# Batch 2 loaded six tokens to a partition and turned on TensorE, batch 4's output turned by the crossbar, an own buffer for one pair's exponentials

## The chip, the cores and the metric

The kernel runs on one core of one Trainium2 chip. Its metric is device time in microseconds (us), the median of several executions. A core has five engines that run their own instruction streams and wait for each other through semaphores: PE (TensorE, matrix products), ACT (ScalarE, activation functions), DVE (VectorE, elementwise work), POOL (GpSimd, here casts and some transfers) and SP (SyncE, here transfers only). Data lies in on-chip memory of 128 partitions; matrix products write to PSUM, 8 banks of 512 fp32 numbers in each partition. Sixteen DMA engines carry out the transfers that SP, ACT and POOL issue.

## The reference

Attention that is causal by blocks of 64 tokens, followed by a feed-forward part with a Swish that has a factor for each of its 2048 channels. There are 8 batches, 8 heads, 576 tokens and a head size of 64:

```python
scores = scale * np.matmul(q, k.transpose(0, 1, 3, 2))
mask = block_i >= block_j                      # blocks of 64 positions
scores = np.where(mask, scores, -1e9); scores -= np.max(scores, axis=-1, keepdims=True)
attn = np.exp(scores); attn /= np.sum(attn, axis=-1, keepdims=True) + 1e-09
x = np.matmul(attn, v).transpose(0, 2, 1, 3).reshape(4608, 512)
h = x @ w_in                                   # 4608 x 2048
out = (h / (1 + np.exp(-beta * h))) @ w_out    # 4608 x 512, fp32
```

Inputs and output are fp32; the kernel computes its products in bf16. Swish is computed as 0.5 h (1 + tanh(beta h / 2)).

## The kernel before

**Two parts, woven together.** Attention works in units of one pair of heads of one batch: 32 units, pair `u = 4 b + c`. The feed-forward part works in nine blocks of 512 tokens (`r` = 0 to 8): for each of 16 groups of 128 channels four products with w_in (line 752), a tanh on ACT (line 762) and one DVE operation that makes `gT` (line 766); then four rows of 128 tokens of 16 products with w_out each (line 785), a scaled copy on ACT (line 797) and a store issued by ACT. A block needs the attention of all its tokens: block 0 that of batch 0, block 4 (tokens 2048 to 2559) that of batches 3 and 4.

**One unit of attention.** The scores are computed transposed, keys in partitions, in four groups (line 620): the two heads use the two halves of PE at the same time. ACT takes the exponentials of each group into a buffer `E` (lines 628 and 640), DVE zeroes the masked corners (634 and 636). Thirty products (664) multiply by V, which has a column of ones that gives the sum. DVE takes the reciprocal (676) and normalizes into `xq` (683). The result, tokens in partitions, must be turned into `xT`, channels in partitions: for batches below `XB` by five PE transposes (708) and copies from PSUM on DVE, for two units of batch 0 on ACT (716 and 718); for batches from `XB` on by DMA transposes through the crossbar, issued on SP (696).

**How Q and K come in.** Both must be turned too, and there are two ways, chosen by `QB`. Batches below `QB` (0 and 1) are loaded with six consecutive tokens to a partition, 96 partitions, one transfer for Q and one for K of each pair (line 545). POOL casts them to bf16 (552), PE turns them in six transposes of 96 columns each (561), and a DVE copy puts the columns in token order (569). Later batches are loaded two pairs at a time, 128 tokens to a step in pieces of 256 bytes (lines 580 and 583, five transfers each for Q and K), cast by POOL (591), and turned by one DMA transpose on SP for the two pairs together (598). V is loaded for a whole batch in six transfers (490 and 493) and cast by POOL (505).

**Weights.** w_in and w_out come in four pieces each, by transfers that POOL issues and that cast to bf16 on the way (lines 451 and 456). These stand in POOL's stream between its casts.

**The order.** Nothing is scheduled on the chip. `Plan.schedule` takes all operations with a duration, dependences, a priority and the buffers they need, runs a list scheduler over them in Python, and writes one fixed stream for each engine with the semaphore waits that the dependences need. Priority is lowest number first; `pr(u)` for attention and `1000 + 100 r` for the feed-forward part make PE fall back on w_in and w_out products when no attention is ready. Buffers are given in the order of that schedule: `E` has three (`NE`), so unit 3 takes the one that unit 0 has finished with; `xq` has two, `QKT` three, `ST` (loaded Q or K) six. Of the PSUM banks, 0 to 3 serve pairs of scores and products with V, 4 to 7 all single-bank work. Products on an identity matrix (469 and 471) fill PE where the plan sees it idle in the first 50 us. SP's stream is a queue too: a transfer that waits for an engine holds all transfers behind it.

Of the kernel before, what the change touches and what calls it, by code (L numbers as in the profile page):

```python
# [338 lines left out]
def bass_blockwise_causal_attn__then__act_swish_beta_kernel(  # L339
# [10 lines left out]
    with es:  # L350
        def sb(name, shape, dt):
            return es.enter_context(nc.sbuf_tensor(name, shape, dt))

        NQ = 2
        QB, XB, CAST = 2, 5, "POOL"
# [10 lines left out]
        Ef = [sb(f"E{i}", [128, 3200], bf16) for i in range(NE)]  # L366
        E3 = [e[:, 0:3072].rearrange("p (c h n) -> p c h n", c=3, h=2) for e in Ef]
# [11 lines left out]
        gT = [sb(f"gT{i}", [128, NJ, RC], bf16) for i in range(2)]  # L379
# [8 lines left out]
        for c, n in (("ST", NS), ("QKn", NQ), ("V", NQ), ("Vs", NQ), ("QKT", 3), ("E", NE), ("inv", 3), ("xq", 2),  # L388
                     ("th", 3), ("gT", 2), ("ost", 3)):
            P.slots(c, n)  # L390
# [7 lines left out]
        def dve_t(n):  # L398
            return (n + 125) / 0.96

# [31 lines left out]
        for i in range(NQ, NE):  # L432
            ones.append(P.op("POOL", 100, mk(lambda g, i=i: g.memset(Ef[i][:, 3136:3200], 0.0)), prio=-4))
# [14 lines left out]
        for a in range(4):  # L448
            def fwi(g, e, a=a):
                n = slice(512 * a, 512 * a + 512)  # L450
                return [g.dma_start(w_in[:, :, n], moe_w_in[:, n].rearrange("(c p) n -> p c n", p=128))]

            win.append(P.op("POOL", 1000, fwi, xfer=3150, dma=(f"d_win{a}", 1), prio=-38.5 if a < 1 else -33.2 if a < 2 else -32))
# [75 lines left out]
        for u in range(NU):  # L529
# [73 lines left out]
            te = P.tile("E")  # L603
            ex = []
            zs = []
            for g0 in range(4):
# [19 lines left out]
                if g0 < 3:  # L626
                    def fe(g, e, ps=ps, g0=g0, te=te):
                        return g.activation(E3[te.slot][:, g0, :, :], PS[:, ps.slot:ps.slot + 2, :], ACT.Exp,  # L628
                                            scale=0.125)
                    x = P.op("ACT", act_t(1024), fe, deps=[o], tiles=[ps, te], lat=act_t(1024) + 93, prio=0)  # L630

                    def fz(g, e, g0=g0, te=te):
                        if g0 < 2:
                            return g.memset(E3[te.slot][64:128, g0, :, 0:64], 0.0)  # L634
                        a = E3[te.slot][64:128, 2, :, 0:64]
                        return g.memset(bass.AP(a.tensor, a.offset, [a.ap[0], [512, 2], [320, 2], [1, 64]]), 0.0)  # L636
                    zs.append(P.op("DVE", 160 if g0 < 2 else 220, fz, deps=[x], tiles=[te], prio=-20))
                else:
                    def fe(g, e, ps=ps, te=te):
                        return g.activation(E4[te.slot][:], PS[:, ps.slot, 0:64], ACT.Exp, scale=0.125)  # L640
                    x = P.op("ACT", act_t(64), fe, deps=[o], tiles=[ps, te], lat=act_t(64) + 93, prio=0)
# [3 lines left out]
            def eblk(te, t, i, h):  # L645
                if t == 4:
                    a = 3072
                elif t == 0 and i == 4:
                    a = 1024 + 512 * h + 448
                else:  # L650
                    g0, off = {0: (0, 0), 1: (1, 0), 2: (2, 0), 3: (2, 320)}[t]
                    a = 1024 * g0 + 512 * h + off + 128 * i - 128 * t
                return Ef[te.slot][:, a:a + 128]
# [13 lines left out]

            av = P.op("PE", 30 * 34, fav, deps=ex + zs + [load[u]], tiles=[te, Tv, pv, ti, tx],
# [72 lines left out]
        for r in range(NRC):  # L741
# [5 lines left out]
            for j in range(NJ):  # L747
# [20 lines left out]
                gs.append(P.op("DVE", dve_t(512), fg, deps=[a], tiles=[ph, tt, tg], prio=0))  # L768
# [107 lines left out]
```

## Time and profile before

| what | us |
|---|---|
| median of 5 executions | 354.76 |
| lowest and highest | 353.71 and 356.17 |
| the profiled execution | 353.5 |
| its span, first to last instruction | 351.7 |
| PE busy | 338.6 (96%) |
| ACT busy | 212.0 (60%) |
| DVE busy | 163.2 (46%) |
| POOL busy | 76.5 (22%) |

The profiled execution is one run among others, 1.3 us under the median. "Busy" of PE contains the fillers on the identity matrix and the overlap of products that follow each other, so that it is not a measure of useful work. Rows in order of time give the start, the duration, the engine, the line of the code and, in brackets, the idle time before and what ended it; "xN" merges N equal instructions. A row with a product fewer than the code has is one whose record is missing.

### The profile page before, as it was taken

How to read it: one execution, taken by the hardware profiler on the slowest of the kernel's cores; microseconds unless marked ns; L12 is line 12 of the kernel's file. 1: busy time of each engine (PE TensorE's matmuls, PEld its weight loads, DVE VectorE, ACT ScalarE, POOL GpSimd, SP SyncE). 2: the span in 40 equal slices, each digit the busy share in tenths (PEclk: the TensorE clock that was granted, in tenths of full speed). 3: DMA queues.
4: the chain of work that ended last, by engine and by line, in shares of the span. 5: the costliest groups of instructions: out<-in, count | busy, mean ns of one | idle time of the engine just before them, and what ended most of it. 6: DMA issues, size and time to landing. Idle time of an engine off the chain costs nothing.

```text
span 351.7 us, 6855 instructions
## 1 busy us (share of the span) xinstructions
PE 338.6 (96%) x2767; PEld 170.6 (49%) x2811; DVE 163.2 (46%) x367; ACT 212.0 (60%) x315; POOL 76.5 (22%) x107
## 2 busy tenths in 40 slices
PE   7898999999999999999999999999999999999997
PEld 5474455435455454445444445444444444444444
DVE  3658694038234565137721474137704803812720
ACT  2937962387476897198872977299616715724721
POOL 7386161053242053151023111400000000000000
PEclk9999999999999999999999999999999999999999
DMA  8999999999999999996679996761111011012003
GB/s 213 215 214 250 208 192 211 242 217 210 201 233 210 219 188 211 230 257 121 136 168 170 193 198 138 184 137 36 32 63 60 0 62 60 0 44 77 1 7 115
DMA packets 146672, 52.05 MB, mean 148 GB/s; under 512 B 134720, under 2 KB 142160, under 8 KB 146640
## 3 DMA queue, kind: packets, MB, share of 16 engines
q1 hardware_dynamic: 137088, 37.97, 53.2%
q10 hardware_dynamic: 5328, 9.44, 7.5%
q0 software_dynamic: 4224, 4.19, 7.3%
q8 instruction: 22, 0.36, 0.4%
q14 instruction: 10, 0.08, 0.1%
HBM read 36.71 MB, written 9.44 MB: 131 GB/s over the span
## 4 chain that ended last, share of the span: by engine, by line
PE 90%; DVE 4%; ACT 2%; issue 2%; POOL 0%; POOLq 0%
PE PS L785 36%; PE PS L752 34%; PE PS L620 8%; PE PS L664 7%; PE PS L708 2%; DVE xq L683 2%; PE PS L469 2%; DVE gT L766 1%; PE PS L471 1%; ACT th L762 1%; ACT E L628 1%; PE PS L561 1%; DVE QKT L569 1%; DVE inv L676 0%; ACT xT L716 0%
## 5 line engine op out<-in xcount | busy, mean ns | idle before, releaser
L752 PE MATMUL PS<-xT,w_in 128*128 128x512 bf16 x550 | 129.4, 379 | 3.7 <-issue 1.0
L766 DVE SCALAR_TENSOR_TENSOR gT<-th,PS 128x512 bf16<-128x512 f32 x144 | 97.0, 684 | 75.4 <-ACT th L762 74.5
L785 PE MATMUL PS<-w_out,gT 128*128 128x512 bf16 (+1 forms) x574 | 129.2, 374 | 1.6 <-issue 1.1
L762 ACT ACTIVATE th<-PS,beta 128x512 f32<-128x512 f32 x144 | 98.0, 706 | 25.4 <-PE PS L752 23.5
L628 ACT ACTIVATE E<-PS 128x1024 bf16<-128x1024 f32 x96 | 96.4, 1038 | 24.1 <-PE PS L620 24.0
L785 PEld LDWEIGHTS PS<-w_out,gT 128*128 128x128 bf16 x592 | 55.1, 98 | 63.5 <-issue 4.5
L752 PEld LDWEIGHTS PS<-xT,w_in 128*128 128x128 bf16 x576 | 52.5, 98 | 64.4 <-DVE gT L766 2.6
L797 ACT ACTIVATE ost<-PS 128x512 f32<-128x512 f32 (+1 forms) x37 | 21.7, 588 | 78.9 <-PE PS L785 78.8
L591 POOL CAST QKn<-ST 128x640 bf16<-128x640 f32 x48 | 34.6, 721 | 49.4 <-DMA ST<-in_k_dram 27.7
L620 PE MATMUL PS<-QKT 64*128 64x320 bf16 (+5 forms) x384 | 39.1, 281 | 1.1 <-DVE xq L683 0.5
L505 POOL CAST Vn<-Vs 128x2560 bf16<-128x2560 f32 (+1 forms) x11 | 19.1, 1740 | 85.4 <-DMA Vs<-in_v_dram 85.3
L664 PEld LDWEIGHTS PS<-Vn,E 128*128 128x128 bf16 x960 | 32.5, 97 | 6.8 <-ACT E L640 0.4
L664 PE MATMUL PS<-Vn,E 128*128 128x65 bf16 x960 | 34.1, 193 | 0.5 <-ACT E L640 0.3
L634 DVE MEMSET E<- 64x64 uint32 x64 | 7.1, 112 | 52.4 <-ACT E L628 50.8
L620 PEld LDWEIGHTS PS<-QKT 64*128 64x128 bf16 (+1 forms) x384 | 13.3, 95 | 29.5 <-issue 13.5
L683 DVE TENSOR_TENSOR xq<-PS,inv 128x640 bf16<-128x640 f32 x32 | 26.3, 823 | 0.9
L569 DVE COPY QKT<-PS 128x576 bf16<-128x576 bf16 x16 | 12.0, 755 | 6.1 <-PE PS L561 6.0
L676 DVE RECIPROCAL inv<-PS 128x10 f32<-128x10 f32 x32 | 7.0, 218 | 15.3 <-PE PS L664 15.0
L552 POOL CAST QKn<-ST 96x768 bf16<-96x768 f32 x14 | 11.8, 846 | 5.0 <-DMA ST<-in_k_dram 3.3
L718 DVE COPY xT<-PS 128x64 bf16<-128x64 bf16 (+2 forms) x40 | 9.6, 286 | 6.3 <-PE PS L708 6.1
L636 DVE MEMSET E<- 64x128 uint32 x32 | 5.3, 165 | 14.3 <-ACT E L628 13.3
L708 PE MATMUL PS<-identB,xq 128*128 128x128 bf16 (+1 forms) x100 | 10.5, 216 | 0.4 <-DVE xq L683 0.2
(33 smaller groups left out, 60.2 us busy)
## 6 DMA issues: line engine op xcount, KB each, us to landing
out_dram<-ost ACTq DMA_DIRECT2D x35, 256.0 KB, 2.4
Vs<-in_v_dram SPq DMA_DIRECT2D x28, 256.0 KB, 4.0
ST<-in_q_dram SPq DMA_DIRECT2D x48, 128.0 KB, 3.1
ST<-in_k_dram SPq DMA_DIRECT2D x48, 128.0 KB, 3.3
ST<-in_q_dram SPq DMA_DIRECT2D x8, 288.0 KB, 5.4
ST<-in_k_dram SPq DMA_DIRECT2D x8, 288.0 KB, 6.3
w_in<-in_moe_w_in_dram POOLq DMA_DIRECT2D x4, 512.0 KB, 11.6
w_out<-in_moe_w_out_dram POOLq DMA_DIRECT2D x4, 512.0 KB, 10.3
```

Source lines behind the costliest of these rows:

```text
L505: return g.tensor_copy(Vn[t.slot][:, :, g0:g1, 0:64], Vs[ts.slot][:, :, g0:g1, :])
L591: return g.tensor_copy(QKn[tn.slot][:].rearrange("p a w n -> p (a w n)")[:, 640 * (2 * a + w):][:, 0:640] .rearrange("p (t h d) -> p t h d ...
L620: z = g.matmul(o, QKT[tqk.slot][r, p, 1, 128 * t:128 * t + m], QKT[tqk.slot][r, p, 0, q0:q1])
L628: return g.activation(E3[te.slot][:, g0, :, :], PS[:, ps.slot:ps.slot + 2, :], ACT.Exp, scale=0.125)
L664: z = g.matmul(o, eblk(te, t, i, h), Vn[Tv.slot][:, t, 2 * c + h, 0:65], start=(t == 0), stop=(t == i))
L683: return g.tensor_tensor(xq[tx.slot][:].rearrange("p i (h d) -> p h i d", h=2), both(pv, 0, 64), x, ALU.mult)
L708: z = g.transpose(PSb[:, px.slot, 128 * i:128 * i + r], xq[tx.slot][0:r, i, :], identB[0:r, 0:r])
L752: z = g.matmul(PS[:, ph.slot, :], w_in[:, c, 128 * j:128 * j + 128], xT[:, c, row % RX:row % RX + RC], start=(c == 0), stop=(c == 3))
L762: return g.activation(th[tt.slot][:], PS[:, ph.slot, :], ACT.Tanh, scale=beta[:, j:j + 1])
L766: return g.scalar_tensor_tensor(out=gT[tg.slot][:, j, :], in0=th[tt.slot][:], scalar=1.0, in1=PS[:, ph.slot, :], op0=ALU.add, op1=ALU.mult)
L785: z = g.matmul(PS[:, po.slot, 0:d1 - d0], gT[tg.slot][:, j, 128 * w:128 * w + 128], w_out[:, j, d0:d1], start=(j == 0), stop=(j == NJ - 1))
L797: return g.activation(ost[to.slot][:, 0:n], PS[:, po.slot, 0:n], ACT.Copy, scale=0.5)
```

## The change

`QB` goes from 2 to 3: batch 2 is loaded and turned like batches 0 and 1. `XB` goes from 5 to 4: the output of batch 4 is turned by DMA transposes. Batch 4's tokens wrap around the ring `xT`, so that each of its units is turned in three pieces. Unit 3 gets its exponentials into a buffer of a new class `EX`, which is the storage of the second `gT`, not used before block 1; the DVE operations of block 1 that write `gT` depend on unit 3's users. The second piece of w_in loses its own priority and is issued with the third and fourth.

```diff
-        QB, XB, CAST = 2, 5, "POOL"
+        QB, XB, CAST = 3, 4, "POOL"
...
+        gT = [sb(f"gT{i}", [128, NJ, RC], bf16) for i in range(2)]
+        Ef.append(gT[1][:].rearrange("p j n -> p (j n)")[:, 0:3200])
...
+        def es_(te):
+            return NE if te.cls == "EX" else te.slot
...
-            win.append(P.op("POOL", 1000, fwi, ..., prio=-38.5 if a < 1 else -33.2 if a < 2 else -32))
+            win.append(P.op("POOL", 1000, fwi, ..., prio=-38.5 if a < 1 else -32))
...
-            te = P.tile("E")
+            te = P.tile("EX" if u == 3 else "E")
...
-                return Ef[te.slot][:, a:a + 128]
+                return Ef[es_(te)][:, a:a + 128]
...
+            if u == 3:
+                spare = te
...
-                gs.append(P.op("DVE", dve_t(512), fg, deps=[a], tiles=[ph, tt, tg], prio=0))
+                gs.append(P.op("DVE", dve_t(512), fg, deps=[a] + (spare.users if r == 1 else []),
+                               tiles=[ph, tt, tg], prio=0))
```

The other lines of the diff index the buffer through `es_`, and POOL zeroes the tail of one buffer more. The plan then makes a new order on every engine. On PE 48 transposes of Q and K are added and 20 of outputs leave; on DVE 8 copies of `QKT` are added and 12 copies of `xT` leave; on SP 12 output transposes are added and two of Q and K leave.

## The prediction

> **What bounds the kernel now.** I read the page's busy times first, then busy time by stretch, then TensorE in order of time, then the waits.
>
> From the page and the busy times by stretch (columns: busy us and instructions of each engine, granted clock, DMA share, GB/s):
>
> ```profile
> PE 338.6 (96%) x2767; PEld 170.6 (49%) x2811; DVE 163.2 (46%) x367; ACT 212.0 (60%) x315; POOL 76.5 (22%) x107
> ...
> 48.73:67.25 18.52, 17.64 (x204) 10.34 (x205) 7.71 (x21) 5.80 (x9) 2.29 (x4) 1.00 1.17 217
> ...
> 119.33:131.00 11.67, 10.82 (x107) 5.55 (x109) 7.32 (x19) 11.33 (x19) 5.20 (x5) 1.00 1.13 214
> ```
>
> TensorE is the bound: 96% busy over the span and 17.64 of 18.52 us even where batch 1 ends, at granted clock 1.00, so I weigh an edit by the TensorE time it adds or takes. Only two things lie outside: the front, before the first product with w_in, and single holes. The DMA engines are full (a share over 1.0), though, so what arrives late there can become a hole. In 119 to 131 ScalarE is busy 11.33 of 11.67 us: there it is nearly the bound.
>
> The front, TensorE and the others in order of time (start, duration, engine, line, count, idle before and what ended it):
>
> ```profile
> 18.00 1.50 POOL L505 CAST Vn<-Vs 128x640 bf16<-128x640 f32 x2 [4.62 <-DMA Vs<-in_v_dram]
> 18.61 1.72 PE L471 MATMUL PS<-identF,identB 64*64 64x256 bf16 x28
> 20.26 1.08 PE L664 MATMUL PS<-Vn,E 128*128 128x65 bf16 x30
> 20.46 0.74 POOL L451 DMA_DIRECT2D w_in<-in_moe_w_in_dram  x1 [0.96 <-DMA Vs<-in_v_dram]
> 21.20 1.52 POOL L505 CAST Vn<-Vs 128x640 bf16<-128x640 f32 x2
> 21.37 0.22 ACT L640 ACTIVATE E<-PS 128x64 bf16<-128x64 f32 x1 [3.74 <-PE PS L664]
> 21.49 2.85 ACT L628 ACTIVATE E<-PS 128x1024 bf16<-128x1024 f32 x3
> 29.25 0.81 PE L752 MATMUL PS<-xT,w_in 128*128 128x512 bf16 x3 [0.41 <-ACT xT L716]
> ```
>
> ScalarE idles 3.74 us until the first product with V (20.26) has freed pair 0's buffer of exponentials, and only then does pair 3's. The first w_in product starts at 29.25.
>
> **The change part by part.** The profiled execution took 353.5 us around a span of 351.7; the median of the five is 354.76, 1.3 above. I work in differences and put them on the median.
>
> *Prices of TensorE blocks*, by the distance of starts in the same order of time:
>
> ```profile
> 33.42 0.43 PE L561 MATMUL PS<-identB,QKn 96*128 96x96 bf16 x6
> 33.69 1.03 PE L752 MATMUL PS<-xT,w_in 128*128 128x512 bf16 x3
> ...
> 70.70 1.03 PE L752 MATMUL PS<-xT,w_in 128*128 128x512 bf16 x4
> 71.56 1.03 PE L785 MATMUL PS<-w_out,gT 128*128 128x512 bf16 x4
> 72.52 0.79 PE L620 MATMUL PS<-QKT 64*128 64x512 bf16 x10
> ...
> 77.66 0.39 PE L620 MATMUL PS<-QKT 64*128 64x448 bf16 x4
> 77.98 1.90 PE L752 MATMUL PS<-xT,w_in 128*128 128x512 bf16 x8
> ...
> 88.57 0.52 PE L708 MATMUL PS<-identB,xq 128*128 128x128 bf16 x5
> 89.02 1.25 PE L785 MATMUL PS<-w_out,gT 128*128 128x512 bf16 x5
> ```
>
> Four products of 512 columns cost 0.86 us (70.70 to 71.56), 0.96 where scores follow (71.56 to 72.52): 0.10 for the turn. Four score products in two halves, 512 columns of stream or 0.215 us, take 0.32 (77.66 to 77.98): 0.11 more. So each visit to the scores costs 0.21 us over its stream. Six transposes of 96 columns cost 0.27, five of an output 0.45.
>
> *Batch 2 turned on TensorE.* Eight groups of six: 8 x 0.27 = +2.2 us, all on the bound, with no cover. *Batch 4's output off it:* 4 x 0.45 = -1.8. *The order:* the plan writes 64 visits to scores after the first w_in product instead of 70: 6 x 0.21 = -1.3. The last counts only if the new visits price like the old; where a visit follows an output's transposes the turn is mostly hidden already (seven such before, four after), so the bound towards nothing is +0.7 and the sum of the three lies between -0.9 and -0.2. I take -0.9, since most visits have the full price.
>
> [...]
>
> *Pair 3's own buffer.* Its exponentials no longer wait for the product at 20.26; they follow pair 2's, which end at 17.63, and are done about 21.1. The second w_in piece moves behind the V casts on POOL, so those end at 20.46 + 1.52 = 22.0 instead of 22.72. Written out by the new order with durations from the rows: products with V of pairs 0 and 1 20.4 to 22.3 (24 fillers instead of 28, one score group more), transposes of pair 0 after its normalization (0.22 + 0.82) to 23.1, pair 2 to 24.0, transposes to 24.5, pair 3 to 25.4, transposes to 25.9, eleven fillers of 0.11 to 27.1, last transposes to 27.5, ScalarE's copy (0.71) to 28.4. First w_in product 28.4 instead of 29.25: -0.85. Bounds: -1.3 if the fillers weren't in the way, 0 if something else holds that product. What is late next: w_in's second piece. Issued at 20.46, at the median landing of w_in (11.6 us) it was there at 32.1 and moves by 1.5; its first user stands near 36.5, so nothing.
>
> *VectorE.* 8 copies of 0.757 more, some 2.7 us of output copies fewer. Four copies (3.0 us) fall at 51 to 56 us between normalizations and output copies, whose users are TensorE's transposes. VectorE is busy only 7.71 of 18.52 us there, but in a chain: last g at 49.7, normalizations (1.04 each) to 51.9, two copies to 53.4, output copies to 54.6. TensorE reaches pair 4's output transposes at 50.4 and waits to 50.9, about 0.5 us. Before, one hole of 0.7 stood at the same place (50.64 to 51.71 for one score group). I count both alike: 0, between -0.7 and +1.
>
> *POOL.* Eight casts of 0.82 for eight of 0.72: +0.8 in 76 us of work. But four of them now stand ahead of three w_out pieces, which so start at 49.3 instead of 45.91 (V of batch 1 cast until 46.0, then 4 x 0.82). The time from issue to landing of w_out's pieces (smallest, median, largest) is in the view of line 456:
>
> ```profile
> DMA to landing us min/median/max: 6.5/10.3/14.3
> ```
>
> The last, issued at 47.4, so landed about 61.7 and would land at 65.1. Its first user stands at 69.5 by my block sums: over 4 us of cover, cost 0; a rival below is what happens without it.
>
> *SP's queue.* 16 loads of 0.51, 4 of 0.60 and 2 turns of 3.93 go (18.5 us of issue), 8 loads of 0.44 and 12 output turns of 1.23 come (18.3). The output turns wait for VectorE, and loads of batches 5 and 6 stand behind them; but those are issued some 20 us ahead of need. The reader of batch 4's rows, the fifth block of 512 tokens, starts near 191, turned at 125 to 149. Cost 0, at most a hole of a few tenths.
>
> *ScalarE.* Same instructions, but products with w_in and scores are packed closer in blocks 1, 3 and 4, while the w_out stretches get longer. 119 to 131 is the row for a dense stretch: the one hole in it was 0.69 us. I take as many holes after as before: 0, between -1.5 and +1.5.
>
> Sum: -0.9 - 0.85 = -1.75, to which a tenth for the lost hole at 30.9 (QKT waits) brings it to -1.85: a profiled time of 351.65, and 354.76 - 1.85 = **352.9 us**. A change under 0.5% (1.8 us) can hardly be told from none in this kernel.
>
> **The rivals.**
>
> *Gain eaten by new holes (same).* The order is planned with given durations; ScalarE's 1038 ns for 1024 columns must then fit by chance. For it: the new order packs blocks 3 and 4 as 119 to 131 is packed now. Against: the stretch with block 5, already so packed (230 to 252), loses only half a microsecond. One hole of 0.7 in each of blocks 1, 3 and 4, less the one that goes at 127: -1.85 + 1.4 = 354.3.
>
> *The edit is empty in front (same).* If the first w_in product waits for something common to both, -0.85 goes: 353.8. For it: TensorE has fillers there, so the place isn't bound by itself. Against: both ScalarE's 3.74 us and the cast order are seen as waits.
>
> *w_out comes late (slower).* The six-token loads of pairs 10 and 11 may share the engines with the three w_out pieces. TensorE's order is fixed, so a late piece stops everything behind it. The last is issued at 50.8, and it decides once it lands after 69.5, that is 18.7 us after issue; every microsecond beyond counts whole. For it: w_in's last piece, beside the six-token loads of batch 1, took 15.3 us instead of 14.3, and the engines were full at 48 to 67 us. At 15.3 there is no hole; at 22 the hole is 3.3 us and the kernel takes 356.2; at twice 14.3 it is 10 us and 362.8. Against: in SP's order V of batch 2 stands before those loads, so most of them come after w_out.
>
> **How the numbers follow.** The sum as worked out, faster: 0.46, own range 350.4 to 353.0. Same, by holes or an empty front: 0.34, 353.0 to 356.2. Late w_out or a like hole: 0.20, 356.2 to 362.8, more likely near the lower end. The low end is every term at its good bound: -0.9 - 1.3 - 0.7 - 1.5 = -4.4, 350.4. The high end, 357.0, takes in the two middle cases and a late piece of up to 2 us.
>
> **What would show it.** The first w_in product at 28.4; ScalarE without a wait of 3.7 us before L640's line; eight more groups of transposes at 0.27; waits of TensorE for the w_out pieces absent (they would disprove the cover); holes after scores in blocks 1, 3 and 4 under 0.7 each. A clock below 1.00, or TensorE waiting for DMA at 60 to 75 us, would make the prediction wrong.

## The result, and the profile after

The changed kernel takes 357.69 us (median of 20 executions, 355.69 to 360.81) where the kernel before takes 354.38 us in the runs beside it: a ratio of 1.0095, with a 95% interval of 1.0076 to 1.0115. It is slower by 0.9%, the sign and the range of the forecast were both missed, and the loss is about twice the half per cent that can just be told from none.

What an execution takes goes with its mean granted clock (the share of full clock that the profile says TensorE was given), which in the profiled one fell by a stretch at half clock (0.50 over 209.85 to 213.20 us, mean 0.995): of the 20, the nine at 0.999 or more have a median of 356.4 us, the other eleven of 358.8; of 88 executions of the kernel before beside the experiments below, 64 and 24, with medians of 354.1 and 356.0. So the change costs 2.3 us where the mean clock is 0.999 or more, and a lower one came more often with it (11 of 20 against 24 of 88).

The profiled execution took 359.43 us around a span of 357.6, that is 5.9 us more than the profiled one of before (353.5); it is 1.7 us above its kernel's median, that one 0.9 below. The page's busy times, granted clock by slice and DMA share by slice:

```profile
PE 341.7 (96%) x2801; PEld 174.1 (49%) x2844; DVE 165.0 (46%) x363; ACT 211.6 (59%) x315; POOL 77.1 (22%) x108
...
PEclk9999999999999999999999989999999999999999
DMA  8979899999898973948899796860121011002003
```

TensorE is still 96% busy and still the bound, but one slice (the 24th, 206 to 215 us) has a clock below full, and the DMA engines, busy from the start, show two dips between 134 and 161 us (a 3 and a 4); before, no slice ahead of 158 us is under 8. (The changed kernel's line numbers are five to seven higher: its lines 625, 669, 759 and 792 are 620, 664, 752 and 785 before, its 603 and 703 are 598 and 696.)

**Where the time went.** I priced every TensorE block after the first w_in product by the prediction's prices (0.216 us a product of 512 columns, 0.265 six transposes of Q and K, 0.09 an output transpose, 0.905 the thirty products with V of a pair, a visit to the scores 0.11 plus a change-over of 0.10, which the prediction calls the turn) and compared the sum with the time from the first w_in product to the last block of w_out. Where scores follow an output's five transposes, the two together cost 0.22 us less: 0.32 or 0.33 from the start of the transposes to that of the scores, where the prices would give 0.45 and 0.10. Two rows of the kernel before:

```profile
128.08 0.52 PE L708 MATMUL PS<-identB,xq 128*128 128x128 bf16 x5
128.40 0.63 PE L620 MATMUL PS<-QKT 64*128 64x320 bf16 x6
```

What the sum leaves over I call holes. The sum is thus counted from the order and priced; only its difference from the measured time is read off the trace.

| profiled execution | first w_in product | sum of blocks | holes | start of the last block |
|---|---|---|---|---|
| before | 29.04 | 300.76 | 5.25 | 335.05 |
| after | 30.72 | 300.48 | 9.81 | 341.01 |

(The first w_in product stands 0.216 us ahead of its first row, since that product's record is missing in both profiles.) So +1.68 us in front, -0.28 in the blocks and +4.56 in holes. The new holes lie in one place. TensorE in order of time there:

```profile
203.16 2.54 PE L759 MATMUL PS<-xT,w_in 128*128 128x512 bf16 x11 [0.16 <-DVE inv L683]
205.54 1.07 PE L669 MATMUL PS<-Vn,E 128*128 128x65 bf16 x30
209.25 0.54 PE L625 MATMUL PS<-QKT 64*128 64x512 bf16 x4 [2.65 <-DMA QKT<-QKn]
209.72 1.84 PE L759 MATMUL PS<-xT,w_in 128*128 128x512 bf16 x4
211.78 1.49 PE L759 MATMUL PS<-xT,w_in 128*128 128x512 bf16 x3 [0.22 <-issue]
```

The scores of pair 26 wait 2.65 us for the Q/K turn, as I call the DMA transpose of Q and K for two pairs (`QKT<-QKn`; an output turn is `xT<-xq`). Then four products of w_in take 1.84 us, nearly twice their usual time (1.03 us for four in the prediction's rows). The two stretches of that place, with the clock ahead of the DMA share:

```profile
200.00:210.00 10.00, 7.19 (x89) 4.19 (x88) 6.58 (x14) 6.57 (x10) 2.88 (x4) 0.99 0.95 197
210.00:220.00 10.00, 9.78 (x51) 3.77 (x51) 3.74 (x10) 8.21 (x14) 0.00 (x0) 0.84 0.95 152
```

The granted clock is 0.84 over 210 to 220 and 0.99 over the 10 us ahead of it; over 209.85 to 213.20 it is 0.50. That makes about 3.4 us of half clock (0.16 and 0.01 of 10 us, at one half). It costs another 1.87 us of holes. Without it, and without the later start that is explained below (1.35), the two profiles are 2.7 us apart, near the 2.3 between the executions at full clock. The gap of 2.65 us was followed by half clock here, and a gap of 2.71 us in another execution of the same kernel (below) was not (granted clock 1.00 from 205 to 220 us); in the run of batch 2 alone (below) one of 2.25 us was (0.50 from 219.30 to 222.60).

Why the turn was late stands on SyncE's queue (issue time, its length, line, count; the second column is how long the issue held the queue):

```profile
130.15 9.62 SPq L703 DMA_TRANSPOSE xT<-xq  x6
139.81 3.09 SPq L603 DMA_TRANSPOSE QKT<-QKn  x1
...
150.86 7.68 SPq L703 DMA_TRANSPOSE xT<-xq  x6
158.59 2.57 SPq L585 DMA_DIRECT2D ST<-in_k_dram  x4
...
197.12 3.30 SPq L585 DMA_DIRECT2D ST<-in_q_dram  x4
200.46 0.62 SPq L588 DMA_DIRECT2D ST<-in_q_dram  x1
201.12 2.25 SPq L585 DMA_DIRECT2D ST<-in_k_dram  x4
203.42 0.60 SPq L588 DMA_DIRECT2D ST<-in_k_dram  x1
204.06 3.46 SPq L603 DMA_TRANSPOSE QKT<-QKn  x1
```

Batch 4's twelve output turns hold SyncE for 17 us in two stretches. In them the DMA engines have less to do: their share is 0.16 over 130 to 140 and 0.41 over 150.86 to 158.54. The turn that pair 26 needs is issued at 204.06 and lands at 209.21; in the kernel before it went out at 198.37 and landed at 204.29, ahead of its first user at 208.22. It is the queue that holds it: POOL's last cast for it ends at 197.61, when SyncE has just begun on the ten loads of the next two pairs (197.12 to 204.02); it issues them one after the other and only then comes to this turn.

The Q/K turns of both kernels, by pairs, show how SyncE's lead came and went (issue time, us):

| pairs | 12, 13 | 14, 15 | 16, 17 | 18, 19 | 20, 21 | 22, 23 | 24, 25 | 26, 27 |
|---|---|---|---|---|---|---|---|---|
| before | 87.64 | 106.77 | 111.73 | 133.67 | 138.38 | 158.12 | 171.64 | 198.37 |
| after | 78.49 | 98.40 | 104.05 | 124.68 | 139.81 | 168.90 | 176.11 | 204.06 |

Up to 125 us the changed kernel is 8 to 9 us ahead, by the issues of batch 2 that it saves SyncE. The output turns use that up and more. Busy times by stretch, of the kernel before:

```profile
100.00:160.00 60.00, 58.15 (x558) 29.57 (x568) 29.10 (x84) 42.77 (x63) 19.04 (x22) 1.00 1.04 220
160.00:260.00 100.00, 98.32 (x855) 48.12 (x869) 47.59 (x110) 67.76 (x100) 14.72 (x16) 1.00 0.63 130
```

And of the changed kernel, the same two stretches:

```profile
100.00:160.00 60.00, 58.89 (x508) 29.21 (x517) 25.58 (x64) 37.20 (x54) 12.37 (x13) 1.00 0.81 168
160.00:260.00 100.00, 95.23 (x816) 47.17 (x826) 45.59 (x106) 68.32 (x104) 17.60 (x20) 0.98 0.72 151
```

The last two columns are the DMA share and GB/s. Before, loads fill the DMA engines until 160 us (1.04, 220 GB/s) and so run ahead of TensorE. After, the share is 0.81 and 168 GB/s there, and loads that were not issued there fall behind 160 us (0.72 and 151 GB/s against 0.63 and 130).

**The front.** The wait of 3.74 us on ScalarE is gone, as forecast (its rows of after):

```profile
18.88 0.22 ACT L645 ACTIVATE gT<-PS 128x64 bf16<-128x64 f32 x1
18.98 2.11 ACT L633 ACTIVATE gT<-PS 128x1024 bf16<-128x1024 f32 x2
```

Yet the first w_in product comes at 30.94 instead of 29.25. TensorE's rows of after:

```profile
5.98 0.69 PE L566 MATMUL PS<-identB,QKn 96*128 96x96 bf16 x6
...
21.83 1.98 PE L669 MATMUL PS<-Vn,E 128*128 128x65 bf16 x60
...
25.07 1.08 PE L669 MATMUL PS<-Vn,E 128*128 128x65 bf16 x30 [0.46 <-DVE xq L690]
...
30.34 0.28 PE L474 MATMUL PS<-identF,identB 128*128 128x256 bf16 x1 [0.33 <-ACT xT L723]
30.94 0.81 PE L759 MATMUL PS<-xT,w_in 128*128 128x512 bf16 x3
```

The first six transposes take 0.69 us at 5.98; in the kernel before they took 0.42 at 5.71. TensorE began this execution more slowly (why is not seen: the granted clock reads 1.00 in both from 5 to 12 us), so that the first scores start at 9.35 instead of 8.00. That is 1.35 of the 1.68 us, and no matter of the change: the profiled executions of all kernels here have their first scores anywhere between 7.96 and 9.35, with the change and without. From the first product with V to the first w_in product it is 9.11 us, before 8.99. The own buffer has given nothing there.

### The profile page after: what moved, and what is told of

Same layout as the page of the kernel before. It is cut to its first block, busy times and chain, and to the rows that moved or that the text cites. A ratio compares the mean times of both kernels' runs of the same rounds, so it can differ in the third digit from the quotient of the medians.

```text
span 357.6 us, 6931 instructions
## 1 busy us (share of the span) xinstructions
PE 341.7 (96%) x2801; PEld 174.1 (49%) x2844; DVE 165.0 (46%) x363; ACT 211.6 (59%) x315; POOL 77.1 (22%) x108
## 4 chain that ended last, share of the span: by engine, by line
PE 79%; DVE 7%; SPq 6%; ACT 4%; issue 2%; DMA 2%; POOL 0%; ACTq 0%; POOLq 0%
PE PS L792 31%; PE PS L759 30%; PE PS L625 6%; PE PS L669 6%; SPq L585 3%; DVE gT L773 2%; SPq L703 2%; PE PS L474 2%; DVE QKT L574 2%; ACT E L633 2%; DVE xq L690 2%; DMA QKT<-QKn 1%; PE PS L715 1%; PE PS L566 1%; ACT th L769 1%
## 5 line engine op out<-in xcount | busy, mean ns | idle before, releaser
L792 PE MATMUL PS<-w_out,gT 128*128 128x512 bf16 (+1 forms) x572 | 127.5, 373 | 1.8 <-issue 0.9
L633 ACT ACTIVATE E<-PS 128x1024 bf16<-128x1024 f32 x93 | 93.3, 1040 | 30.2 <-PE PS L625 30.0
L625 PE MATMUL PS<-QKT 64*64 64x64 bf16 (+5 forms) x384 | 37.6, 281 | 3.3 <-DMA QKT<-QKn 2.9
L596 POOL CAST QKn<-ST 128x640 bf16<-128x640 f32 x40 | 28.8, 720 | 45.7 <-DMA ST<-in_k_dram 25.2
L669 PEld LDWEIGHTS PS<-Vn,E 128*128 128x128 bf16 x930 | 31.3, 97 | 6.3 <-DVE xq L690 0.6
L669 PE MATMUL PS<-Vn,E 128*128 128x65 bf16 x930 | 32.7, 193 | 0.5 <-DVE xq L690 0.5
L625 PEld LDWEIGHTS PS<-QKT 64*128 64x128 bf16 (+1 forms) x384 | 13.4, 95 | 31.2 <-issue 10.8
L574 DVE COPY QKT<-PS 128x576 bf16<-128x576 bf16 x24 | 17.9, 753 | 9.2 <-PE PS L566 8.8
L557 POOL CAST QKn<-ST 96x768 bf16<-96x768 f32 x22 | 18.1, 825 | 5.7 <-DMA ST<-in_k_dram 3.7
L474 PE MATMUL PS<-identF,identB 128*128 128x256 bf16 x51 | 9.5, 338 | 3.4 <-POOL identF L415 2.4
L725 DVE COPY xT<-PS 128x512 bf16<-128x512 bf16 (+1 forms) x28 | 7.1, 300 | 6.5 <-PE PS L715 6.5
```

Of the source, the lines that this page charges most:

```text
L574: return g.tensor_copy(QKT[td.slot][:, p, w, 0:576].rearrange("c (p j) -> c p j", j=6), PSb[:, pt.slot, 0:576].rearrange("c (j p) -> c p j ...
L596: return g.tensor_copy(QKn[tn.slot][:].rearrange("p a w n -> p (a w n)")[:, 640 * (2 * a + w):][:, 0:640] .rearrange("p (t h d) -> p t h d ...
L625: z = g.matmul(o, QKT[tqk.slot][r, p, 1, 128 * t:128 * t + m], QKT[tqk.slot][r, p, 0, q0:q1])
L633: return g.activation(E3[es_(te)][:, g0, :, :], PS[:, ps.slot:ps.slot + 2, :], ACT.Exp, scale=0.125)
L669: z = g.matmul(o, eblk(te, t, i, h), Vn[Tv.slot][:, t, 2 * c + h, 0:65], start=(t == 0), stop=(t == i))
L792: z = g.matmul(PS[:, po.slot, 0:d1 - d0], gT[tg.slot][:, j, 128 * w:128 * w + 128], w_out[:, j, d0:d1], start=(j == 0), stop=(j == NJ - 1))
```

## The experiments

Two theories went in. **S:** SyncE's one in-order queue is late in the second half, since batch 4's output turns stand in it ahead of loads and Q/K turns. **E:** the loss is early, batch 2 on TensorE. Beside them: any new order brings such accidents. In all tables "holes" and "sum" are those of the profile, by the prices above; they are of one execution, the time is the median of several.

### One part alone

> The changed kernel with batch 4's output turned on TensorE again (XB 5); batch 2 on TensorE and the own buffer stay. Theory S (SP's stream is full, and batch 4's twelve output turns, 17.3 us of it in the profile of the changed kernel, make the turn of pairs 26 and 27 late, which gives a hole of 2.65 us and a TensorE clock of one half for 3.4 us after it): no wait of TensorE for a DMA over 1 us, granted clock 1.00, 353.0 to 354.5 us. Rival E (the loss comes early, from batch 2 on TensorE: VectorE's chain of copies at 50 to 60 us and a front that is 1.7 us later): the time stays at 356 or above. Rival O (any new order of the plan is as likely to be worse): no forecast for the hole, 354 to 358.

```diff
 (changed kernel)
-        QB, XB, CAST = 3, 4, "POOL"
+        QB, XB, CAST = 3, 5, "POOL"
```

> The kernel before with batch 4's output turned by the crossbar (XB 4) and nothing else. Theory S: SP has the twelve output turns more and none of batch 2's turns and loads less, so the turns of Q and K of batches 5 to 7 come late; TensorE waits for them by 2 to 6 us in all, 356.5 to 361 us. Rival E: no early change, so 354 to 355 us. Rival O: 354 to 358 with no wait for the turns.

```diff
 (kernel before)
-        QB, XB, CAST = 2, 5, "POOL"
+        QB, XB, CAST = 2, 4, "POOL"
```

> Batches as in the kernel before (QB 2, XB 5) with the own buffer for pair 3 and the later second w_in piece alone. Theory S: SP as before, no new hole; the first w_in product stands 0.5 to 0.9 us earlier against the transposes of pair 0 than before, 353.3 to 354.3 us. Rival E: 354.4, or later if the front that starts later is the buffer's doing. Rival O: 354 to 358.

```diff
 (changed kernel)
-        QB, XB, CAST = 3, 4, "POOL"
+        QB, XB, CAST = 2, 5, "POOL"
```

> The kernel before with batch 2 loaded six tokens to a partition and turned on TensorE (QB 3), output of batch 4 on TensorE, no own buffer. Theory S: 2.2 us more of transposes on TensorE, less the visits to scores that the order saves; SP has less to issue; no wait for turns of Q and K over 1 us, 354 to 355.5 us. Rival E: this alone brings the loss, 356.5 us or above. Rival O: 354 to 358.

```diff
 (kernel before)
-        QB, XB, CAST = 2, 5, "POOL"
+        QB, XB, CAST = 3, 5, "POOL"
```

| what is left of the change | median us | ratio [95%] | sum | holes |
|---|---|---|---|---|
| batch 2 on PE and the buffer (first) | 358.44 | 1.0106 [1.0076, 1.0137] | 302.70 | 7.69 |
| batch 4 by crossbar (second) | 360.15 | 1.0163 [1.0129, 1.0196] | 298.97 | 12.34 |
| buffer and w_in order (third) | 355.53 | 1.0019 [0.9993, 1.0045] | 300.97 | 5.82 |
| batch 2 on PE (fourth) | 357.72 | 1.0095 [1.0063, 1.0126] | 301.85 | 10.23 |

The kernel before beside them took 354.74. The fourth's profile is of an execution of 363.56 us, 5.8 above the median, with a granted clock of 0.986; its holes contain 3.4 us at half clock and are not those of the median. The buffer alone is worth nothing that can be measured. Batch 4 by the crossbar alone takes 1.8 us out of the sum, as priced, and is the slowest: its holes more than double. The waits of TensorE (time, times, longest) in that kernel:

```profile
PE PS L620 <- DMA QKT<-QKn: 5.1, 3, 2.7
```

So S holds there. It did not hold in the first as written: with batch 4 back on TensorE the time did not come back. Its TensorE rows:

```profile
216.06 1.06 PE L669 MATMUL PS<-Vn,E 128*128 128x65 bf16 x30 [1.12 <-ACT E L633]
...
221.84 1.06 PE L669 MATMUL PS<-Vn,E 128*128 128x65 bf16 x30 [0.83 <-DMA xT<-xq]
```

The product with V waits because both buffers of normalized output (`xq`) are held by output turns not yet through (the first row names ScalarE, which had long been done; the output turn landed at 215.97). The fourth shows the same wait, 2.2 us in one piece, in its one long execution. So with batch 2 on TensorE the sum is up by 1 to 2 us, as E has it, and TensorE waits for output turns instead of Q/K turns. E is part of the truth and S not yet in its right form.

### More turns, or fewer loads on SyncE

> The changed kernel with XB 3: batch 3's output too goes by the crossbar. TensorE's blocks lose another 4 visits of 0.45 us (-1.8 us in the sum of blocks); SyncE's queue gains about 12 output turns of 1.2 us, some 15 us, from about 105 us on. Theory S (SyncE's one in-order queue is late in the second half, and the Q/K turn of pairs 26 and 27 landed 2.7 us late for it): the holes in TensorE after a Q/K turn or an output turn grow by more than the blocks shrink; 358.5 to 362 us, and TensorE waits for DMA at two or more places for over 1 us each. Rival P (the loss of the changed kernel is one accident of order at 205 to 212 us, half clock included): the accident is not repeated, and the shorter sum of blocks shows: 353.5 to 355.5 us.

```diff
 (changed kernel)
-        QB, XB, CAST = 3, 4, "POOL"
+        QB, XB, CAST = 3, 3, "POOL"
```

365.93 us, 1.0329 [1.0269, 1.0389]; sum 299.96, holes 18.72. TensorE's longest waits:

```profile
PE PS L625 <- DMA QKT<-QKn: 8.7, 3, 4.3
```

The blocks shrink by 0.5 us (I had expected 1.8; there are four visits to the scores more) and the holes grow by 8.9. Of these 5.8 are waits for Q/K turns (2.9 in the changed kernel); most of the rest is half clock behind them (granted 0.83 over 140 to 150 us and 0.66 over 180 to 190, 0.986 over this execution, 0.995 there). The loss goes beyond the range that I had given. Against a mere accident of order this speaks plainly: more output turns, later Q/K turns.

> The changed kernel, with the V loads of batches 3 to 7 issued by GpSimd's queue instead of SyncE's: 30 issues of about 0.56 us (some 3.4 us for each batch, 17 us in all) leave SyncE's stream from about 115 us on; no other part of the change is undone. Theory S: the Q/K turns of the later batches are issued earlier and land ahead of use; the holes of 2.71 us at 206 to 209 us and the half clock behind it go, and the time is that of the kernel before or better, 352.5 to 355.5 us. Rival T (batch 2 on TensorE costs its 2 us and the crossbar for batch 4 gives little back, whatever SyncE does): 356.5 to 358.5 us with no hole over 1 us. Rival G (GpSimd becomes late with the Q/K casts, since each of its issues takes longer than SyncE's): over 358 us, and the turns now wait for casts.

> The kernel before, with the V loads of batches 3 to 7 issued by GpSimd's queue instead of SyncE's, as a control for the run of the changed kernel with the same edit. If SyncE is not late in the kernel before (its Q/K turns land 1.3 to 15 us ahead of their first use), freeing it is worth nothing: 353.8 to 355.5 us, ratio 0.998 to 1.002. If SyncE's queue holds the kernel before as well, through the small holes at 126 us (0.63 us) and others, it is faster by up to 1 us: 353 to 354. If GpSimd gets late with its casts: over 356 us.

```diff
 (changed kernel; the same two lines in the kernel before)
-                    vs.append(P.op("SP", 300 + 550 * n, fv, tiles=[ts],
+                    vs.append(P.op("SP" if b < 3 else "POOL", 300 + 550 * n if b < 3 else 1000, fv, tiles=[ts],
...
-                                   dma=["d_V", h0, 1]))
+                                   dma=["d_V", h0 if b < 3 else "p", 1]))
```

368.03 us (1.0392 [1.0320, 1.0464]) and 365.24 us (1.0315 [1.0266, 1.0363]): far slower, both. The remedy was worse than the illness, and rival G's cause, late casts, does not explain it: SyncE's Q/K turns wait for GpSimd's casts 14.3 us in all in the changed kernel with this edit (10.9 without) and 10.4 in the kernel before with it (15.1 without). In the changed kernel with this edit the Q/K turns need, from issue to landing (smallest, median, largest):

```profile
L603 SPq DMA_TRANSPOSE QKT<-QKn x10: 3016/4014/5896, 78.7 to 229.6; - x10
...
DMA to landing us min/median/max: 5.0/7.6/14.8
```

In the changed kernel the same row reads 5.0/6.1/7.3. The turn of 14.8 us was issued at 197.31, 2.3 us after V loads began to go out from GpSimd, and everything that SyncE or ScalarE issued from 201 to 206 us took 9 to 10 us to land. What the transfers of the two queues do to each other in the DMA engines no run here separates. These two therefore say nothing for or against S; they say only that SyncE's queue is not relieved that way.

### The turns later in the order

> The changed kernel with three buffers instead of two for the normalized output (xq) and with the output turns placed 5 us later in the written order, so that SyncE reaches them when their data is there. SyncE issues the same transfers, none is taken away. Theory S in the form that SyncE's queue stands blocked at an output turn (issue spans of 9.62 us for six at 130.15 and of 7.68 us for six at 150.86, at 1.23 us unblocked) with the loads of later batches behind it: these spans shrink to under 8 us for six, the later loads go out earlier, the hole at 206 to 209 us shrinks below 1 us; 353.5 to 356 us. Theory S in the form that the sheer issue time of SyncE is the bound: the hole stays or moves, 356.5 to 359 us. Rival P (an accident of order): a new order, with no hole: also 354 to 356 us, but without shorter issue spans of the output turns.

```diff
 (changed kernel)
-        xq = [sb(f"xq{i}", [128, 5, 128], bf16) for i in range(2)]
+        xq = [sb(f"xq{i}", [128, 5, 128], bf16) for i in range(3)]
...    ("xq", 2) becomes ("xq", 3)
             m = P.op("DVE", dve_t(640), fm, deps=[av, r], tiles=[pv, ti, tx], prio=0,
+                     lat=dve_t(640) + 5000 * (b >= XB))
```

356.82 us, 1.0080 [1.0039, 1.0121]: above what S had given for it (353.5 to 356), in the range of the other form, which had the hole stay. No wait for a DMA is left on TensorE: holes 5.73, 0.5 above the kernel before (the profile is of an execution of 359.90 us; its half clock, granted 0.50 over 15 to 20 us and 0.85 over 20 to 25, lies ahead of the first w_in product, outside of sum and holes). But its order has 72 visits to the scores where the changed kernel has 64, and the sum is 301.94.

The two edits one at a time, on the changed kernel:

> The changed kernel with the third buffer of normalized output alone; SyncE's list of instructions is the changed kernel's, word for word, and TensorE's order changes a little. Theory S (SyncE stands blocked at output turns that were placed before their data is there): the issue spans at about 130 and 151 us keep their length, the Q/K turn of pairs 26 and 27 is late again, the time stays at 356.5 to 358.5 us, so what mended the run with late turns was their place. Rival B (the third buffer did it, by not holding TensorE's product with V): the hole goes and the time is 355.5 to 357 us.

```diff
 (changed kernel: the third buffer alone)
-        xq = [sb(f"xq{i}", [128, 5, 128], bf16) for i in range(2)]
+        xq = [sb(f"xq{i}", [128, 5, 128], bf16) for i in range(3)]
```

> The changed kernel with its output turns placed 5 us later and two buffers of normalized output; with three buffers and the same place it took 356.82 us, with three buffers alone 359.55 us. Theory S: the issue spans of 9.62 and 7.68 us at 130 and 151 us shrink, and no Q/K turn is late by over 1 us: 356 to 357.5 us. If two buffers make TensorE's product with V wait for the turns: holes at the product with V, 357.5 to 360 us.

```diff
 (changed kernel: the later place alone)
+                     lat=dve_t(640) + 5000 * (b >= XB))
```

The third buffer alone: 359.55 us, 1.0132 [1.0099, 1.0164], the same stall of 2.86 us at 206 and 1.86 behind it (holes 10.01), and a time 1 us above the range given; SyncE again issues the twelve output turns six at a time. The later place alone: 358.66 us, 1.0135 [1.0084, 1.0185], holes 8.48 (profiled at 361.73 us, at a mean granted clock of 0.991). With two buffers the product with V now waits for the turns:

```profile
PE PS L669 <- DMA xT<-xq: 1.9, 2, 1.2
PE PS L625 <- DMA QKT<-QKn: 0.7, 1, 0.7
```

So it takes both: the later place brings the Q/K turn in time, and the third buffer pays for the later place. To see whether this is also worth time, the changed kernel and the one with both edits side by side on one chip:

> The changed kernel itself, side by side with the run of three buffers and late output turns on one chip: 357 to 358.5 us. Theory S expects the Q/K turn of pairs 26 and 27 to be late again at about 206 us.

> The changed kernel with three buffers of normalized output and the output turns placed 5 us later, side by side with the changed kernel. Its stalls behind SyncE were gone in the first profile, 4.1 us by the holes, but its order had eight visits to the scores more (1.5 us at 0.21 with the turns): theory S expects 1 to 2.5 us less than the changed kernel, 355.3 to 357 us. If the time of the changed kernel does not hang on that stall, no difference: both within 0.6 us.

The changed kernel again: 357.88 us, 1.0089 [1.0052, 1.0126]. With both edits: 356.59 us, 1.0066 [1.0034, 1.0099]. The difference, 1.3 us, is in the range that S had given (stall 2.8, visits 1.5 the other way); the two intervals overlap, so the time alone does not prove it. The profiles show the mechanism. The changed kernel has the stall again, without the half clock behind it this time (granted clock 1.00 over 205 to 220 us):

```profile
210.07 0.54 PE L625 MATMUL PS<-QKT 64*128 64x512 bf16 x4 [2.71 <-DMA QKT<-QKn]
210.54 1.90 PE L759 MATMUL PS<-xT,w_in 128*128 128x512 bf16 x8
```

With both edits TensorE runs without a gap there:

```profile
207.44 1.06 PE L669 MATMUL PS<-Vn,E 128*128 128x65 bf16 x30
208.34 1.03 PE L759 MATMUL PS<-xT,w_in 128*128 128x512 bf16 x4
209.30 0.22 PE L625 MATMUL PS<-QKT 64*64 64x64 bf16 x2
```

Between these two profiles the holes shrink by 2.5 us and the sum grows by 1.5; the rest of the 2.3 us between them lies ahead of the first w_in product, where the changed kernel's execution had a granted clock of 0.56 to 0.59 from 14 to 18 us.

SyncE's queue with both edits, its DMA transposes from 125 to 160 us:

```profile
129.74 4.96 SPq L703 DMA_TRANSPOSE xT<-xq  x3
134.74 3.14 SPq L603 DMA_TRANSPOSE QKT<-QKn  x1
137.92 3.81 SPq L703 DMA_TRANSPOSE xT<-xq  x3
...
149.87 4.31 SPq L703 DMA_TRANSPOSE xT<-xq  x3
...
157.50 3.84 SPq L703 DMA_TRANSPOSE xT<-xq  x3
```

The twelve turns go out three at a time, with loads and a Q/K turn between them, instead of six. The turn for pairs 26 and 27 is now issued at 196.71 instead of 204.06. What SyncE did from 100 us to that issue, summed from its issue rows:

| us | before | changed | both edits |
|---|---|---|---|
| Q and K loads | 41.2 (69) | 37.1 (60) | 33.5 (55) |
| V loads | 12.7 (18) | 11.6 (16) | 10.2 (16) |
| Q/K turns | 24.8 (6) | 20.9 (6) | 21.1 (6) |
| output turns | 10.5 (8) | 26.1 (20) | 27.3 (20) |
| standing, and steps between | 9.2 | 8.4 | 4.7 |
| the turn is issued at | 198.37 | 204.06 | 196.71 |

The numbers in brackets count the issues. The changed kernel loses 15.6 us to the twelve output turns and gets 9.9 back elsewhere, most of it since it was ahead at 100 us and has nine loads of Q and K fewer left to issue: 5.7 us late. S as first written, "SyncE stands blocked", is only half of it: the twelve turns themselves hold the queue for over 1.2 us each whether blocked or not, and both edits gain their 7.3 us half by less standing (3.7) and half by five loads that no longer stand ahead of this turn (3.6).

### The other two settings with late turns

> The changed kernel with batch 4's output on TensorE (XB 5), three buffers of normalized output and the output turns of batches 5 to 7 placed 5 us later; so batch 2 on TensorE and the own buffer are what is left of the change. Without the two last edits this took 358.44 us, with 1.9 us more in the sum of TensorE's blocks than before and 2.3 us in two waits for output turns. Theory S: the two waits go, the sum stays; 356.0 to 357.2 us, which is what batch 2 on TensorE costs by itself. Rival: the waits come from the crossbar being slow, not from SyncE's order, and stay: 357.8 to 359 us.

```diff
 (changed kernel, both edits above)
-        QB, XB, CAST = 3, 4, "POOL"
+        QB, XB, CAST = 3, 5, "POOL"
```

357.78 us, 1.0105 [1.0078, 1.0131], on the same chip as the pair above; holes 5.45, no wait for a DMA, clock 1.000. Here nothing is left to stall, and it is as slow as the changed kernel: the sum is 303.53, 2.77 above the kernel before. That is the price of batch 2 on TensorE by itself: eight groups of transposes, 2.12, and three visits to scores fewer (5 instead of 8, against 300.75 of the kernel before with both edits) that an output transpose hides, 0.66. The time came out 0.6 us above my range; the earlier holes (20 to 100 us) grew too, from 1.9 us, in the kernel before with both edits, to 3.6. One of them, TensorE waiting for VectorE's copy of a turn, in the changed kernel:

```profile
36.86 0.54 PE L625 MATMUL PS<-QKT 64*128 64x448 bf16 x6
38.25 0.59 PE L759 MATMUL PS<-xT,w_in 128*128 128x512 bf16 x2 [0.85 <-DVE QKT L574]
```

Set beside the kernel with both edits and XB 4 (356.59), batch 4's output by the crossbar is worth some 1.2 us once its turns do not stall anything (the two intervals overlap); in the blocks it is 1.59.

> The kernel before with batch 4's output by the crossbar (XB 4, batch 2 still by the crossbar), and with three buffers of normalized output and the output turns placed 5 us later. Without the two last edits this took 360.15 us, with a sum of TensorE's blocks 1.8 us below the kernel before and 7.1 us more of holes. Theory S: the holes were SyncE standing at the output turns; without it they fall to the 5 to 6 us of the kernel before, the shorter sum shows, and the time is 352.3 to 354.0 us, faster than the kernel before. Theory S in the form of sheer load (SyncE and the DMA engines have no room for batch 4's turns as well, however they are placed): holes over 1 us stay, 356 to 360 us.

```diff
 (kernel before, both edits above)
-        QB, XB, CAST = 2, 5, "POOL"
+        QB, XB, CAST = 2, 4, "POOL"
```

363.03 us, 1.0241 [1.0216, 1.0265]: what I hoped would beat the kernel before is slower still, and beyond the range of the form "sheer load" too. The sum is 300.02, the holes 11.00, with one of 4.74 us at the scores behind the last Q/K turn. TensorE's rows:

```profile
244.56 1.06 PE L664 MATMUL PS<-Vn,E 128*128 128x65 bf16 x30
250.36 0.25 PE L620 MATMUL PS<-QKT 64*64 64x64 bf16 x4 [4.74 <-DMA QKT<-QKn]
```

SyncE's rows just before:

```profile
234.68 4.63 SPq L580 DMA_DIRECT2D ST<-in_k_dram  x4
239.35 0.60 SPq L583 DMA_DIRECT2D ST<-in_k_dram  x1
239.99 5.14 SPq L696 DMA_TRANSPOSE xT<-xq  x4
245.18 3.08 SPq L598 DMA_TRANSPOSE QKT<-QKn  x1
```

The last turn goes out at 245.18; in the kernel before at 227.74. Four output turns stand just ahead of it, as in the kernel before; the whole queue is 17 us later, and twelve output turns at 1.23 us are 15. With batch 2 and batch 4 both on the crossbar SyncE was late in both placements tried, the early one (360.15) and this one. So S has two forms, and each is seen: sheer load with twelve turns of Q and K and 36 of outputs, the place with ten of Q and K.

### The edits on the kernel before

> The kernel before, with three buffers of normalized output and its output turns (batches 5 to 7) placed 5 us later in the written order. Theory S: the kernel before lost little to its own blocked stretch at 161 to 167 us, since its Q/K turns land 1.3 to 15 us ahead; 353.8 to 355.3 us, ratio 0.997 to 1.002. Should the edit be good in itself by 1 us or more, 353.5 us or less, then what it gains on the changed kernel is not all from the late turn.

> The kernel before with three buffers of normalized output and its output turns placed 5 us later, once more, for a narrower interval: it took 352.85 us and 0.9963 [0.9945, 0.9980] in six runs. If it is faster than the kernel before, the ratio lies at 0.994 to 0.998 again with an interval below 1; if the six runs were luck, at 0.998 to 1.001.

> The kernel before with its output turns placed 5 us later and the two buffers of normalized output that it has; the run with three buffers and the same place took 352.85 us. Theory S (the place is what pays): 352.3 to 353.6 us. If with two buffers TensorE's product with V has to wait for a turn that is now later, a hole of 0.3 to 1 us at two or three places: 354 to 356.5 us, and then it takes both edits.

> The kernel before with the third buffer of normalized output alone. Theory S: the buffer is worth nothing where the product with V is not held by the two, 354 to 355.3 us, ratio 0.998 to 1.002; if the gain of the run with both edits came from the buffer, 352.5 to 353.6 us.

```diff
 (kernel before; the first two have both, the third only the line with lat, the fourth only those of xq)
-        xq = [sb(f"xq{i}", [128, 5, 128], bf16) for i in range(2)]
+        xq = [sb(f"xq{i}", [128, 5, 128], bf16) for i in range(3)]
...    ("xq", 2) becomes ("xq", 3)
             m = P.op("DVE", dve_t(640), fm, deps=[av, r], tiles=[pv, ti, tx], prio=0,
+                     lat=dve_t(640) + 5000 * (b >= XB))
```

Both edits: first 352.85 us, 0.9963 [0.9945, 0.9980] in six runs, then, on another chip, 354.59 us, 1.0024 [0.9999, 1.0050] in twelve. The later place alone 355.08 us, 1.0022 [0.9997, 1.0046]; the buffer alone 354.70 us, 0.9991 [0.9952, 1.0029]. The gain did not come back, so there is none to be claimed, and what was expected of the place alone (352.3 to 353.6) did not come either. The kernel before loses nothing measurable by the place of its output turns, as S has it, and no version here is shown to beat it.

## Why the prediction was wrong

The step that failed is SP's queue: "Cost 0, at most a hole of a few tenths". Its sum was right as a sum, 18.5 us of issue going and 18.3 coming. But what went lay ahead of 100 us, where the DMA engines are full (a share of 1.06 over 20 to 100 in the changed kernel, 1.07 before), and only about half of it was gained: the Q/K turns up to 125 us go out 8 to 9 us earlier. What came lay at 130 to 158 us, where SyncE issues little else for 17 us while the DMA share falls to 0.16; it took this lead and more, so that the next turns go out 1.4, 10.8, 4.5 and 5.7 us late. Why not all of the 18.5 us was gained no run here separates. The loads were indeed issued ahead of need in the kernel before, but the step took the loads' lead for the lead of what decides: the Q/K turn behind them. That one stood 3.9 us ahead of its user (landed 204.29, used 208.22); it went out 5.7 us later and landed 4.9 us later, and TensorE was ready for it 1.6 us earlier (at 206.6). A hole of 2.65 us and, in the profiled execution, 1.87 us more at the half clock behind it were the price. The fault was to add up one queue over its whole length.

At full clock the change costs 2.3 us where -1.85 was forecast. Of these 4.1 us the hole is 2.65; the front (0.85) and the blocks (0.62) below are the rest.

The other terms:

- **Blocks, -0.9:** -0.28 by the counts and prices above, within the bounds given (-0.9 to -0.2), at their poor end. Batch 4's transposes off TensorE are -1.8, batch 2's on it +2.1; the visits to scores fell to 64 as counted, -1.26; but three visits fewer stand behind an output's transposes, +0.66. I had named these seven and four and then not counted them: of the six visits that went, three had cost next to nothing. The granted clock stayed at 1.00 from 28 to 100 us, where batch 2's transposes are.
- **Front, -0.85:** nothing, 9.11 against 8.99 us from the first product with V to w_in; the run of the buffer alone, at 1.0019 [0.9993, 1.0045], agrees. The 3.74 us on ScalarE went, as seen above, but the chain on TensorE that I had written out took 3.24 us between the products of pairs 0 and 2, not 2.7, waiting for VectorE's normalization (0.46), and the end waits for ScalarE's copy (0.33). The rival "the edit is empty in front" was right in this term.
- **VectorE, 0:** about right. At 40 to 60 us the holes are 0.6 us against 1.2 before, while one of 0.85 us came at 37.
- **w_out late:** did not happen; TensorE never waits for a piece of w_out. The cover of 4 us held.
- **ScalarE, 0:** the holes at 120 to 160 us sank from 1.4 to 0.4.

The slower side had 0.20 and was given to w_out's pieces "or a like hole". A like hole it was, but at 206 us instead of 60 to 75. As for what the change is worth by itself: with both edits it has no stall and is still 0.66% [0.34, 0.99] slower. It pays 2.8 us of blocks for batch 2, gets 1.6 back for batch 4, and gets nothing for the buffer; that is 1.2 of the 2.3 us, and its holes are 0.5 higher than before, the rest is not placed. Undoing the stall, with the eight visits that this costs, is worth the other 1.3 us of the changed kernel's 3.6 on that chip. What stays open is why one execution had the half clock behind the stall (2.65 us) and another not (2.71), and why GpSimd's V loads slow the turns so much.

## What to carry to other kernels

Add up a queue by stretches and against the engines behind it: here 18.5 us of issue taken away where the DMA engines are full bought a lead of 8 to 9 us, and 17 us added where loads had been filling a lead took that away and was felt some 50 us later. For each late transfer compare the lead of the thing that is last in its chain, here the DMA transpose behind load and cast, not that of the loads. A gain of a third of a per cent in a few executions on one chip has to be timed again on another chip before it is believed.

## What the runs showed that was not expected

- The DMA transposes of an output's pieces (128 by 512 and less) hold SyncE for 1.23 us each (median of 36), and in the two stretches in which six of them go out in a row the DMA engines are at 0.16 and 0.41 of their time: what these turns cost here is the issue.
- A gap of 2.65 us on TensorE was followed by half clock for some 3.4 us, and so was one of 2.25 us in the run of batch 2 alone (granted clock 0.50 from 219.30 to 222.60); one of 2.71 us was not (1.00 from 205 to 220).
- V loads from GpSimd's queue beside SyncE's turns stretched a Q/K turn of the changed kernel to 14.8 us where 7.3 us was the longest without, and the edit made both kernels 10 to 11 us slower.
- One and the same kernel against the same kernel before came out at 0.9963 [0.9945, 0.9980] and at 1.0024 [0.9999, 1.0050] on two chips: an interval from few executions on one chip is too narrow by that much.
